# Attention and two MoE layers on one core: first loads in smaller pieces, the first GEMM by column halves, a new order table

## The chip, the core and the metric

The kernel runs on one core of a Trainium2 chip. The metric is the device time of one execution in microseconds: 537.37 us before the change, the median of 3 runs (537.26 to 537.60). In the text PE is the matmul engine, DVE the vector engine, ACT the scalar engine, POOL GpSimd, and SP the engine that issues the DMAs.

## The reference

Three layers follow each other on 1152 tokens (2 batches of 576) of width 512.

```python
# attention: 8 heads of 64; heads 0-3 see 32 keys back, heads 4-7 every 4th of 128 keys back
attn = softmax(where(mask, q @ k.T / 8, -1e9)) @ v
# layer 1: w_in 512x1024 and w_out 1024x512, both float64
h = x @ w_in
solu = h * softmax(h)
x = (solu - mean) / sqrt(var + 1e-6) * g_ln @ w_out
# layer 2: 4 experts, w1 512x1024 and w2 1024x512, float32
out = sum_e p[:, e] * (relu(x @ w1[e]) @ w2[e])
```

## The kernel before

**Attention.** A unit is one batch and one third of the positions of 4 heads: P units for the plain mask, D units for the dilated one, 12 units in all. `att_U` (L238) works a unit in 12 steps. PE puts the mask and 24 small products into a PSUM tile `pa` (the scores, L245 and L254). DVE takes the maximum (L262) and subtracts it (L264), ACT takes the exponent (L267), DVE the sum (L269) and its reciprocal (L271), and POOL or DVE the product into `pd` (L273). PE transposes `pd` (L279), ACT or DVE copies it (`pt`), PE multiplies it with the values (AV, L292), and the result is split into a rounded part `xhi` and a rest `xlo` (L308, L311). A D unit needs a third of `qkD`, which one load of 1168 KB brings.

**Weights.** `load_in` brings float64 weights `w_in`; `conv_in` turns a piece into float32 and splits it into `wh` and `wl`: two ACT passes, three DVE or POOL passes (`convert`, L169), a cast (`copy`) and a subtraction (L206). `w_in` comes in 128-row pieces: `draw0` in two halves of 512 columns, the other three whole. `load_out` and `conv_out` do the same for `w_out`.

**The first GEMM.** `moe_H` (L315) multiplies 128 tokens with all 1024 columns: for each of 4 row pieces `kk` three products (hi*hi, hi*lo, lo*hi) on both column halves, 24 matmuls into one PSUM tile `pm`. DVE then takes the row maximum (`nmx`, L326), ACT the exponent, and so on; `moe_T` (L340) transposes, `moe_X` (L359) is the second GEMM. Two `pm` and two `pa` tiles exist. Layer 2 (`up`, `down`, from L486) is unrolled by loops at the end, whose order the change leaves alone.

**The order.** Every engine executes its instructions in the order of the code. Up to the first expert's half that order is written out in the table `ORDER`: each word takes one generator one step further (`UP.t.b` and `UD.t.b` units, `lP`, `lD`, `lvp`, `lvd` loads of q, k and v, `lI` and `VI` loads and conversions of `w_in`, `lO` and `VO` of `w_out`, `H`, `T`, `X` the GEMM steps). A `+` moves the step's free choices to other engines: in `copy` from ACT to DVE, in `pick` between DVE and POOL. All loads are issued by SP in that order; a load waits there when its buffer is in use or when one of 8 DMA queues still has the load of eight before.

**The end.** `down` (L539) computes 128 tokens of the result; the last tile is cut into two column pieces of 256, so that the first can be stored while the second is computed. Both pieces are halves of one PSUM tile `po`.

## Time and profile before

| | us |
|---|---|
| median of 3 runs | 537.37 |
| the profiled execution | 536.57 |
| its span, first to last instruction | 534.8 |
| around the span | 1.77 |
| PE busy | 520.2 |
| DVE busy | 349.6 |
| ACT busy | 198.9 |
| POOL busy | 166.8 |

The span is divided into 40 slices of 13.4 us on the page; PE is below nine tenths in the first one alone. The costs below come from the profiled execution, which is 0.80 us shorter than the median run. A timeline row gives start, duration, engine, line, the operation and what ended the idle time before it.

### The profile page before, as it was taken

The numbers are of one execution on the slowest core, as the hardware profiler recorded it, in microseconds if no ns is written. First come the engines' busy times: TensorE is split into PE (matmuls) and PEld (weight loads), VectorE is DVE, ScalarE is ACT, GpSimd is POOL, SyncE is SP. The second block draws the span as 40 slices with busy tenths as digits, with TensorE's granted clock in tenths as the row PEclk, the third lists the DMA queues.
The fourth block names the chain that finished last, engine by engine and source line by source line (L and its number), as shares of the span: only waits on it lengthen the run. The fifth ranks groups of instructions, "written<-read, shape, count | busy, mean of one in ns | idle before, by whom it ended". The sixth has DMA issues, their size and how long they took to land.

```text
span 534.8 us, 8713 instructions
## 1 busy us (share of the span) xinstructions
PE 520.2 (97%) x3660; PEld 465.8 (87%) x3660; DVE 349.6 (65%) x472; ACT 198.9 (37%) x302; POOL 166.8 (31%) x121
## 2 busy tenths in 40 slices
PE   4899999999999999999999999999999999999997
PEld 2668789889999898988989898898989889898986
DVE  6999995373889974865585386568538646853532
ACT  3877892445246231421332242133124213412200
POOL 3672320001002111731382173138217413820300
PEclk9999999999999999999999999999999999999999
DMA  8962140000132300500310040031005002000022
GB/s 326 406 214 101 64 135 1 0 1 20 60 132 65 119 2 0 159 1 0 98 60 1 1 157 1 0 102 58 1 1 158 0 1 79 1 1 0 2 80 97
DMA packets 16856, 36.21 MB, mean 68 GB/s; under 512 B 3376, under 2 KB 3632, under 8 KB 16176
## 3 DMA queue, kind: packets, MB, share of 16 engines
q1 hardware_dynamic: 16816, 35.65, 19.1%
q8 instruction: 29, 0.48, 0.4%
q14 instruction: 11, 0.09, 0.1%
HBM read 33.28 MB, written 2.36 MB: 67 GB/s over the span
## 4 chain that ended last, share of the span: by engine, by line
PE 94%; DMA 2%; DVE 2%; ACT 1%; issue 0%; SPq 0%; DVEq 0%; ACTq 0%
PE pm L553 18%; PE pa L553 18%; PE pm L483 17%; PE pa L483 17%; PE pm L321 10%; PE pm L370 8%; PE pa L292 2%; PE pa L349 2%; DMA draw<-in_moe_w_in_dram 2%; PE pa L279 1%; DMA rw<-in_moe_w_dram 1%; PE pa L254 1%; ACT pt L159 0%; DVE sm L264 0%; PE pa L245 0%
## 5 line engine op out<-in xcount | busy, mean ns | idle before, releaser
L496 DVE SCALAR_TENSOR_TENSOR hl<-ct,hh 128x512 fp32r<-128x512 f32 (+1 forms) x64 | 61.5, 980 | 32.4 <-ACT hh L494 32.4
L494 ACT ACTIVATE hh<-ct 128x512 fp32r<-128x512 f32 (+1 forms) x64 | 42.2, 682 | 51.9 <-DVE ct L526 22.9
L553 PE MATMUL pm<-wh,hh 128*128 128x512 f32 (+1 forms) x148 | 56.9, 384 | 0.6 <-DVE xf L558 0.6
L483 PE MATMUL pa<-xoh,hl 128*128 128x256 f32 (+1 forms) x192 | 56.9, 296 | 0.0
L483 PE MATMUL pm<-xoh,hl 128*128 128x256 f32 (+1 forms) x192 | 56.8, 296 | 0.0
L483 PE MATMUL pm<-xol,hh 128*128 128x256 f32 (+1 forms) x192 | 56.8, 296 | 0.0
L483 PE MATMUL pa<-xol,hh 128*128 128x256 f32 (+1 forms) x192 | 56.8, 296 | 0.0
L553 PE MATMUL pm<-wl,hh 128*128 128x512 f32 (+1 forms) x148 | 56.8, 384 | 0.0
L483 PE MATMUL pm<-xoh,hh 128*128 128x256 f32 (+1 forms) x192 | 56.8, 296 | 0.0
L483 PE MATMUL pa<-xoh,hh 128*128 128x256 f32 (+1 forms) x192 | 56.8, 296 | 0.0
L553 PE MATMUL pm<-wh,hl 128*128 128x512 f32 (+1 forms) x148 | 56.7, 383 | 0.0
L553 PE MATMUL pa<-wl,hh 128*128 128x512 f32 x144 | 56.1, 390 | 0.0
L553 PE MATMUL pa<-wh,hh 128*128 128x512 f32 x144 | 56.1, 390 | 0.0
L553 PE MATMUL pa<-wh,hl 128*128 128x512 f32 x144 | 56.0, 389 | 0.0
L510 POOL TENSOR_TENSOR ct<-ct,ct 128x512 f32<-128x512 f32 (+1 forms) x15 | 22.4, 1492 | 78.7 <-ACT ct L508 52.6
L402 POOL TENSOR_TENSOR wl<-wl,wh 128x1024 fp32r<-128x1024 f32 x7 | 16.9, 2413 | 95.7 <-ACT wh L159 95.7
L558 DVE SCALAR_TENSOR_TENSOR xf<-pm,pr,xf 128x512 f32<-128x512 f32 (+1 forms) x33 | 24.1, 730 | 32.9 <-PE pm L553 32.9
L159 ACT CAST wh<-wl 128x1024 fp32r<-128x1024 f32 x16 | 16.8, 1053 | 71.0 <-PE pa L553 40.6
L558 DVE SCALAR_TENSOR_TENSOR xf<-pa,pr,xf 128x512 f32<-128x512 f32 x31 | 23.1, 746 | 29.4 <-PE pa L553 29.4
L483 PEld LDWEIGHTS pm<-xoh,hh 128*128 128x128 f32 x192 | 36.4, 190 | 0.3
L483 PEld LDWEIGHTS pm<-xol,hh 128*128 128x128 f32 x192 | 36.4, 190 | 0.3
L483 PEld LDWEIGHTS pa<-xol,hh 128*128 128x128 f32 x192 | 36.4, 190 | 0.3
(180 smaller groups left out, 1252.6 us busy)
## 6 DMA issues: line engine op xcount, KB each, us to landing
wl<-in_moe_w_dram SPq DMA_DIRECT2D x16, 512.0 KB, 4.2
...
out_dram<-xf SPq DMA_DIRECT2D x8, 256.0 KB, 2.0
...
```

Source lines behind the costliest of these rows:

```text
L159: nc.scalar.copy(out, in_)
L292: nc.tensor.matmul(po[64 * row:64 * row + 64, 0, o:o + 96], lhsT=vv, rhs=pt[:, j, :, g, :], start=True, stop=True)
L321: nc.tensor.matmul(pm[:, n, :], lhsT=xx[:, kk, cols], rhs=ww["in", kk][:, 512 * n:512 * n + 512], start=(n_ == 0 and i < 2), stop=(n_ == K ...
L349: nc.tensor.transpose(pa[:, f // 4, (f % 4) * 128:(f % 4) * 128 + 128], e[:, f // 4, (f % 4) * 128:(f % 4) * 128 + 128], ident)
L370: nc.tensor.matmul(pm[:, dd, 0:CW], lhsT=w_, rhs=x_[:, f, :], start=(f == 0 and i == 0), stop=(f == KF - 1 and i == 2))
L402: pick().tensor_tensor(out=out, in0=a, in1=b, op=op)
L483: nc.tensor.matmul(ps[:, ff, 0:n], lhsT=a[:, kk, fc], rhs=b[:, kk, :], start=kk == 0 and m == 0, stop=kk == 1 and m == 2)
L494: nc.scalar.activation(out=hv, in_=src, func=AF.Relu)
L496: nc.vector.scalar_tensor_tensor(out=lv, in0=src, scalar=0.0, in1=hv.bitcast(F32), op0=ALU.max, op1=ALU.subtract)
L510: poolv().tensor_tensor(out=c12, in0=c21, in1=c22, op=ALU.add)
L553: nc.tensor.matmul(po[:, u, 0:dn], lhsT=h_[:, f, cols], rhs=w_, start=(f == 0 and i == 0), stop=(f == 3 and i == 2))
L558: nc.vector.scalar_tensor_tensor(out=acc[:, t, dc], in0=po[:, u, 0:dn], scalar=pr[:, t, e:e + 1], in1=acc[:, t, dc], op0=ALU.mult, op1=ALU ...
```

## The change

- Every load goes through `load`, which makes it wait until all but the last 2,000,000 bytes of the loads before it have landed.
- The q and k of D units come by thirds (459 KB each, overlap included), those of P units also by thirds; `w_in` comes in 8 pieces of 128x512 (524 KB each), each with buffers of its own; the converted pieces rotate through 4 buffers, the raw `w_out` pieces through 2.
- `moe_H` finishes columns 0 to 511 over all four `kk` before it begins columns 512 to 1023; a step is 3 matmuls instead of 6.
- `keep_busy` puts 4 bf16 matmuls of a zero tile, 512 columns each, behind the scores of the first P and the first D unit. The zero tile is set on DVE; the three `pd` tiles are set to zero on POOL instead of DVE.
- The last output tile is cut into 384 and 128 columns, in two PSUM tiles from different pools.
- `g_ln` and the expert weights `probs` are laid out by partition before the launch, so that their loads are no longer made of elements of 4 and 16 bytes.
- `ORDER` is another table.

```diff
-KORD = (0, 1, 2, 3)
-HCUT = (1, 1, 2, 2, 4, 2, 4, 4, 4)
-XCUT = (2, 2, 4)
+HCUT = (1, 1, 1, 1, 2, 2, 2, 4, 4)
+XCUT = (1, 1, 2)
 NEG = -8.0e9
+AHEAD = 2000000
...
-lI.0 lP.0.0 VI.0 lD.0 VI.0 UP.0.0 VI.0 UD.0.0 VI.0 UP.0.0 UP.0.0 UD.0.0 lI.4 lP.1.0 VI.4 UP.0.0 UD.0.0 UP.0.0 lI.1 UP.0.0 UD.1.0 UD.1.0 lI.2 VI.0+
...
+lP.0.0 UP.0.0 UP.0.0 UP.0.0 UP.0.0 UP.0.0 UP.0.0 lD.0.0 UD.0.0 wu.4 wu.4 wu.4 wu.4 UP.0.0 lI.3 VI.3 VI.3 UD.0.0 UD.0.0 UD.0.0 UP.0.0 UP.0.0
...
+    wz = const.tile([128, 512], BF16, name="wz")
+    nc.vector.memset(wz.bitcast(U32), 0)
+    wps = psm.tile([128, 2, 512], F32, name="pm", tag="pm")
...
-    cv = at.enter_context(tc.tile_pool(name="cv", bufs=1))
+    cvp = at.enter_context(tc.tile_pool(name="cvp", bufs=4))
+    crp = at.enter_context(tc.tile_pool(name="crp", bufs=2))
...
-    QP, QD = 2 * TH, 2 * S
+    QP, QD = 2 * TH, 4 * 96
...
-        qkD.append(p.tile([128, QD + 32 + 2 * S], F32, name=f"qkD{b}", tag=f"qkD{b}"))
+        qkD.append(p.tile([128, 3, QD + 4 * 128], F32, name=f"qkD{b}", tag=f"qkD{b}"))
...
-        nc.vector.memset(pd, 0.0)
+        nc.gpsimd.memset(pd, 0.0)
...
+    loads = []
+
+    def load(out, in_):
+        i = nc.sync.dma_start(out=out, in_=in_).ins
+        n = mybir.dt.size(out.dtype)
+        for d in out.shape:
+            n *= d
+        loads.append((i.name, n))
+        total = 0
+        for k in range(len(loads) - 1, -1, -1):
+            total += loads[k][1]
+            if total > AHEAD:
+                info = mybir.DependencyInfo(mybir.DependencyClass.Sync, mybir.DependencyReason.DATA)
+                tc.add_manual_dep(i, loads[k][0], info, reason="bytes on the way")
+                break
...
     def load_qk(quad, t, b):
         if quad == "D":
-            nc.sync.dma_start(out=qkD[b], in_=qkd[b])
+            load(out=qkD[b][:, t], in_=qkd[b, :, t])
         else:
-            ts = slice(0, 1) if t == 0 else slice(1, 3)
-            nc.sync.dma_start(out=qkP[b][:, ts], in_=qkp[b, :, ts])
+            load(out=qkP[b][:, t], in_=qkp[b, :, t])
...
+    def keep_busy(n):
+        for i in range(n):
+            nc.tensor.matmul(wps[:, i % 2, :], lhsT=wz[:, 0:128], rhs=wz, start=True, stop=True)
+            yield
...
     def load_in(j):
         j, half = j % 4, j // 4
-        if half:
-            nc.sync.dma_start(out=dins[j][:, 1024:2048].bitcast(I64), in_=w_in[128 * j:128 * j + 128, 512:1024])
-            return
-        r = dins[j] = erp.tile([128, 2048], I32, name=f"draw{j}", tag=f"draw{j}")
-        n = 512 if j == 0 else 1024
-        nc.sync.dma_start(out=r[:, 0:2 * n].bitcast(I64), in_=w_in[128 * j:128 * j + 128, 0:n])
+        r = dins[j, half] = erp.tile([128, 1024], I32, name=f"draw{j}{half}", tag=f"draw{j}{half}")
+        load(out=r.bitcast(I64), in_=w_in[128 * j:128 * j + 128, 512 * half:512 * half + 512])
 
     def conv_in(j):
         j, half = j % 4, j // 4
-        sl = slice(512 * half, 512 * half + (512 if j == 0 else 1024))
+        sl = slice(512 * half, 512 * half + 512)
         if ("in", j) not in whi:
             whi["in", j] = wp.tile([128, 1024], F32R, name=f"wh{j}", tag=f"wh{j}")
             wlo["in", j] = wp.tile([128, 1024], F32R, name=f"wl{j}", tag=f"wl{j}")
-        a = (erp.tile([128, 1024], F32, name="eva", tag="eva") if j % 2 else cva)[:, sl]
-        yield from convert(dins[j][:, 2 * sl.start:2 * sl.stop], a)
+        a = cvp.tile([128, 512], F32, name="cva", tag="cva")
+        yield from convert(dins[j, half], a)
...
     def load_out(j, t):
-        nc.sync.dma_start(out=cvr[:, 1024 * t:1024 * t + 1024].bitcast(I64), in_=w_out[256 * j + 128 * t:256 * j + 128 * t + 128, :])
+        r = douts[j, t] = crp.tile([128, 1024], I32, name="cvr", tag="cvr")
+        load(out=r.bitcast(I64), in_=w_out[256 * j + 128 * t:256 * j + 128 * t + 128, :])
...
-            qt, kt, hq, hk, mi = qkD[b][:, 0:QD], qkD[b][:, QD:], S // 2, S // 2, (1, 2, 0)[t]
+            qt, kt, hq, hk, mi = qkD[b][:, t, 0:QD], qkD[b][:, t, QD:], 96, 128, (1, 2, 0)[t]
...
-        for n_, kk in enumerate(KORD):
-            seq = [(xhi, whi, n) for n in range(2)] + [(xhi, wlo, n) for n in range(2)] + [(xlo, whi, n) for n in range(2)]
-            for i, (xx, ww, n) in enumerate(seq):
-                nc.tensor.matmul(pm[:, n, :], lhsT=xx[:, kk, cols], rhs=ww["in", kk][:, 512 * n:512 * n + 512],
-                                 start=(n_ == 0 and i < 2), stop=(n_ == KD - 1 and i >= 4))
-            if n_ % HCUT[t] == HCUT[t] - 1:
-                yield
+        for n in range(2):
+            for kk in range(KD):
+                for i, (xx, ww) in enumerate(((xhi, whi), (xhi, wlo), (xlo, whi))):
+                    nc.tensor.matmul(pm[:, n, :], lhsT=xx[:, kk, cols], rhs=ww["in", kk][:, 512 * n:512 * n + 512],
+                                     start=(kk == 0 and i == 0), stop=(kk == KD - 1 and i == 2))
+                if (n * KD + kk) % HCUT[t] == HCUT[t] - 1:
+                    yield
...
-        po = pair(g % 2 + t + (0 if t < 4 else 1))
-        cuts = ((0, 256), (256, 256)) if last and t == NTT - 1 else ((0, 512),)
+        k = g % 2 + t + (0 if t < 4 else 1)
+        cuts = ((0, 384), (384, 128)) if last and t == NTT - 1 else ((0, 512),)
...
+            po = pair(k + u)[:, 0, 0:dn]
...
-        nc.sync.dma_start(out=g_sb, in_=g_ln.rearrange("(f p) -> p f", p=128))
-        nc.sync.dma_start(out=pr_raw, in_=probs.rearrange("(t p) e -> p t e", p=128))
+        load(out=g_sb, in_=g_ln)
+        load(out=pr_raw, in_=probs.rearrange("p (t e) -> p t e", t=NTT))
```

The table's effect on the queues. PE at the very start; `pa` tiles hold scores, transposes and AV results, `wz` is the zero tile. Before:

```order
L254 MATMUL pa_163<-qkP0_103 32x64 x24
...
L254 MATMUL pa_191<-qkD0_104 32x64 x24
...
L254 MATMUL pa_233<-qkD0_104 32x64 x24
...
L254 MATMUL pa_272<-qkP0_103 32x64 x24
...
L254 MATMUL pa_309<-qkD0_104 32x64 x24
L279 MATMUL pa_339<-ident_69,pd0_109 128x128 x6
```

After:

```order
L282 MATMUL pa_160<-qkP0_109 32x64 x24
...
L282 MATMUL pa_194<-qkD0_110 32x64 x24
...
L172 MATMUL pm_71<-wz_69 128x512
L307 MATMUL pa_237<-ident_72,pd0_115 128x128 x6
...
L282 MATMUL pa_253<-qkP0_109 32x64 x24
L320 MATMUL pa_295<-pt_244,vp_291 64x96 x8
...
L282 MATMUL pa_313<-qkD0_110 32x64 x24
```

Before, five units' scores stand ahead of the first transposes; now two, with the zero matmuls between, and the first AV stands ahead of the fourth unit's scores.

DVE just ahead of the row maximum of token tile 0 (`nmx` from the tile's `pm`); `cva` and `eva` are converted pieces, `wl` their rests, `st` and `sm` belong to a unit's softmax. Before:

```order
L262 TENSOR_REDUCE st_664<-pa_594 128x6
L271 RECIPROCAL st_507<-st_507 128x6
L264 TENSOR_TENSOR sm2_114<-pa_594,st_664 128x6x64
L273 TENSOR_TENSOR pd0_109<-sm0_112,st_507 128x6x64
L231 TENSOR_TENSOR xlo_87<-pa_641,xhi_86 128x2x2x96
L271 RECIPROCAL st_621<-st_621 128x6
L326 TENSOR_REDUCE nmx_79<-pm_447 128x1
```

After:

```order
L290 TENSOR_REDUCE st_714<-pa_686 128x6
L292 TENSOR_TENSOR sm1_119<-pa_686,st_714 128x6x64
L231 TENSOR_TENSOR wl2_341<-cva_652,wh2_340 128x512
L188 CAST xhi_89<-pa_730 128x2x192
L259 TENSOR_TENSOR xlo_90<-pa_730,xhi_89 128x2x192
L297 TENSOR_REDUCE st_714<-sm1_119 128x6
L299 RECIPROCAL st_714<-st_714 128x6
L259 TENSOR_TENSOR xlo_90<-pa_748,xhi_89 128x2x192
L354 TENSOR_REDUCE nmx_82<-pm_460 128x1
```

Two more units' results stand ahead of that maximum now, and the last pieces of `w_in`. Counted over the whole queues up to that point:

| | before | after |
|---|---|---|
| PE up to tile 0's last matmul: units with scores / transposes / AV | 9 / 5 / 5 | 9 / 7 / 7 |
| PE: matmuls of tile 0, of tile 1, zero matmuls | 24, 12, 0 | 24, 18, 4 |
| DVE up to tile 0's maximum: first maximum, subtraction / sum, reciprocal | 9 / 8 | 9 / 8 |
| DVE: `xlo` subtractions (by units) / `xhi` casts / `pt` copies | 5 / 0 / 1 | 7 / 2 / 0 |
| DVE: half pieces of `w_in` through the first two passes | 8 | 8 |
| DVE: the third pass / `wh` cast / `wl` subtraction, in half pieces | 0 / 0 / 4 | 3 / 1 / 5 |
| DVE: zeroing of `pd` | 3 | 0 |

DVE at the handover from the first GEMM to layer 2; `hl` is the rest of a transposed tile that the last second-GEMM group needs, `ct` and `sw` are the first sums of layer 2. Before:

```order
L231 TENSOR_TENSOR hl_1419<-pa_1498,hh_1418 128x8x128
L402 TENSOR_TENSOR ct0_1581<-xf_1236 128x2x256
L402 TENSOR_TENSOR sw0_1590<-rw0_1543,rw1_1545 128x2x256
L231 TENSOR_TENSOR hl_1419<-pa_1489,hh_1418 128x8x128
L157 CAST hh_1586<-rw0_1543 128x512
```

After:

```order
L188 CAST hh_1443<-pa_1554 128x8x128
L259 TENSOR_TENSOR hl_1444<-pa_1554,hh_1443 128x8x128
L188 CAST hh_1443<-pa_1566 128x8x128
L259 TENSOR_TENSOR hl_1444<-pa_1566,hh_1443 128x8x128
L188 COPY xf_1313<-pm_1498 128x2x384
```

Before, a sum that reads a load of `w1` stands between the two `hl`; now each cast and its `hl` follow each other, and the loads' readers come later.

## Rows read from the trace of the kernel before

**Rows 1.** Windows: length, busy PE PEld DVE ACT POOL, PE clock, DMA share, GB/s.
```profile
6.47:40.56 34.09, 29.27 (x561) 20.92 (x549) 29.71 (x57) 23.82 (x36) 20.92 (x13) 1.00 0.87 327
40.56:94.70 54.14, 54.14 (x518) 46.67 (x517) 45.08 (x76) 37.54 (x60) 11.26 (x10) 1.00 0.22 74
135.00:140.00 5.00, 4.29 (x25) 3.97 (x24) 4.67 (x8) 1.75 (x2) 0.00 (x0) 1.00 0.18 67
...
0.00:30.00 30.00, 20.05 (x437) 14.28 (x438) 24.05 (x52) 18.90 (x27) 16.58 (x27) 1.00 0.95 371
30.00:130.00 100.00, 99.92 (x867) 85.59 (x866) 71.58 (x113) 61.00 (x94) 18.49 (x14) 1.00 0.18 56
```

**Rows 2.** Timeline of PE: scores, AV, transposes, scores, tile 0's last matmuls.
```profile
18.14 0.97 PE L254 MATMUL pa<-qkP 64*32 64x64 f32 x48
...
20.50 0.88 PE L292 MATMUL pa<-pt,vp 128*64 128x96 f32 x16
...
23.64 0.82 PE L279 MATMUL pa<-ident,pd 128*128 128x128 f32 x6
...
26.14 0.72 PE L254 MATMUL pa<-qkP 64*32 64x64 f32 x48
...
39.89 0.63 PE L321 MATMUL pm<-wh,xlo 128*128 128x512 f32 x2
```

**Rows 3.** Timeline of ACT and POOL: the first piece of w_in, first and last pass.
```profile
4.41 0.67 ACT L173 ACTIVATE draw<-draw 128x512 int32<-128x512 uint32 x1 [2.39 <-DMA draw<-in_moe_w_in_dram]
...
12.65 1.27 POOL L206 TENSOR_TENSOR wl<-cva,wh 128x512 fp32r<-128x512 f32 x1 [3.68 <-ACT wh L159]
```

**Rows 4.** DVE by line: count, ns minimum/median/maximum, first and last start; then its timeline.
```profile
L231 DVE TENSOR_TENSOR xlo<-pa,xhi x14: 497/546/887, 22.4 to 94.7; 128x384 fp32r<-128x384 f32 x10, 128x192 fp32r<-128x192 f32 x4
...
L157 DVE COPY pt<-pa x1: 957/957/957, 17.7 to 17.7; 128x768 f32<-128x768 f32 x1
...
L181 DVE CUSTOM_DVE_ANT_0 cva<-cvr,cva x3: 680/685/693, 74.7 to 82.9; 128x1024 uint16<-128x1024 uint16 x3
...
L206 DVE TENSOR_TENSOR wl<-eva,wh x1: 1210/1210/1210, 27.2 to 27.2; 128x1024 fp32r<-128x1024 f32 x1
...
6.47 0.36 DVE L177 TENSOR_SCALAR cva<-cva 128x512 uint32<-128x512 uint32 x1
...
10.17 0.56 DVE L262 TENSOR_REDUCE st<-pa 128x6 f32<-128x384 f32 x1 [1.56 <-PE pa L254]
...
14.31 0.68 DVE L177 TENSOR_SCALAR cva<-cva 128x512 uint32<-128x512 uint32 x1
...
40.56 1.22 DVE L326 TENSOR_REDUCE nmx<-pm 128x1 f32<-128x1024 f32 x1
```

**Rows 5.** The chain that ended last, two pieces; then PE's one wait there.
```profile
65.55 5.47 PE pm L321 x24
...
138.40 16.74 PE pm L370 x95
...
PE pm L370 <- DVE hl L231: 0.7, 1, 0.7
```

**Rows 6.** The end: transposes (chain), PE and DVE timeline, stores with us to landing.
```profile
127.44 1.76 PE pa L349 x16
...
527.69 0.28 PE L553 MATMUL pm<-wh,hh 128*128 128x256 f32 x1
527.89 0.75 DVE L558 SCALAR_TENSOR_TENSOR xf<-pa,pr,xf 128x512 f32<-128x512 f32 x1 [1.97 <-PE pa L553]
529.86 0.39 PE L553 MATMUL pm<-wh,hh 128*128 128x256 f32 x1 [0.58 <-DVE xf L558]
531.59 0.48 DVE L558 SCALAR_TENSOR_TENSOR xf<-pm,pr,xf 128x256 f32<-128x256 f32 x1 [1.78 <-PE pm L553]
...
out_dram<-xf SPq DMA_DIRECT2D x8, 256.0 KB, 2.0
out_dram<-xf SPq DMA_DIRECT2D x2, 128.0 KB, 1.7
```

More of the change, by code (lines that the diff above doesn't have):

```diff
@@ L141, in load_vp @@
         vps[u, b] = t
-        nc.sync.dma_start(out=t.rearrange("p c h d -> p (c h d)"), in_=vpw[b, :, u])
+        load(out=t.rearrange("p c h d -> p (c h d)"), in_=vpw[b, :, u])
+    def keep_busy(n):
+        for i in range(n):
+            nc.tensor.matmul(wps[:, i % 2, :], lhsT=wz[:, 0:128], rhs=wz, start=True, stop=True)
+            yield
     whi, wlo = {}, {}
@@ L165, in fused_kernel @@
     wpo = [None]
-    cvr = cv.tile([128, 2048], I32, name="cvr", tag="cvr")
-    cva = cv.tile([128, 1024], F32, name="cva", tag="cva")
     def convert(raw, a):
@@ L206, in conv_in @@
         pick().tensor_tensor(out=lo, in0=a, in1=hi.bitcast(F32), op=ALU.subtract)
+    douts = {}
     def load_out(j, t):
-        nc.sync.dma_start(out=cvr[:, 1024 * t:1024 * t + 1024].bitcast(I64), in_=w_out[256 * j + 128 * t:256 * j + 128 * t + 128, :])
+        r = douts[j, t] = crp.tile([128, 1024], I32, name="cvr", tag="cvr")
+        load(out=r.bitcast(I64), in_=w_out[256 * j + 128 * t:256 * j + 128 * t + 128, :])
     def conv_out(j, t):
         sl = slice(512 * t, 512 * t + 512)
-        a = cva[:, sl]
-        yield from convert(cvr[:, 1024 * t:1024 * t + 1024], a)
+        a = cvp.tile([128, 512], F32, name="cva", tag="cva")
+        yield from convert(douts[j, t], a)
         if ("out", j) not in whi:
@@ L388, in load_w1 @@
             r = r.rearrange("p (t f) -> p t f", t=2)
-            nc.sync.dma_start(out=r, in_=w1[e, 256 * kh:256 * kh + 256, 512 * fh:512 * fh + 512].rearrange("(t p) f -> p t f", p=128))
+            load(out=r, in_=w1[e, 256 * kh:256 * kh + 256, 512 * fh:512 * fh + 512].rearrange("(t p) f -> p t f", p=128))
             w1raw[g].append(r)
@@ L397, in load_w2 @@
             f0 = 512 * fh + 256 * j
-            nc.sync.dma_start(out=r, in_=w2[e, f0:f0 + 256, :].rearrange("(t p) f -> p t f", p=128))
+            load(out=r, in_=w2[e, f0:f0 + 256, :].rearrange("(t p) f -> p t f", p=128))
             w2raw[g].append(r)
@@ L487, in up @@
         _, n, _ = SCH[s]
-        hh, hl = hb[s]
         k = g % 2 + (s if g else 1 - s)
@@ L552, in down @@
                 for i, (h_, w_) in enumerate(((hh, wh), (hh, wl), (hl, wh))):
-                    nc.tensor.matmul(po[:, u, 0:dn], lhsT=h_[:, f, cols], rhs=w_, start=(f == 0 and i == 0), stop=(f == 3 and i == 2))
+                    nc.tensor.matmul(po, lhsT=h_[:, f, cols], rhs=w_, start=(f == 0 and i == 0), stop=(f == 3 and i == 2))
             yield
             if g == 0:
-                nc.vector.tensor_scalar(out=acc[:, t, dc], in0=po[:, u, 0:dn], scalar1=pr[:, t, e:e + 1], scalar2=None, op0=ALU.mult)
+                nc.vector.tensor_scalar(out=acc[:, t, dc], in0=po, scalar1=pr[:, t, e:e + 1], scalar2=None, op0=ALU.mult)
             else:
-                nc.vector.scalar_tensor_tensor(out=acc[:, t, dc], in0=po[:, u, 0:dn], scalar=pr[:, t, e:e + 1], in1=acc[:, t, dc],
+                nc.vector.scalar_tensor_tensor(out=acc[:, t, dc], in0=po, scalar=pr[:, t, e:e + 1], in1=acc[:, t, dc],
                                                op0=ALU.mult, op1=ALU.add)
@@ L689, in _lay_out @@
         d[name] = a[:, at].reshape(b, 128, 3, 8 * n)
+    d["moe_g_ln"] = d["moe_g_ln"].reshape(-1, 128).T
+    p = d["moe2_domain_probs"]
+    d["moe2_domain_probs"] = p.reshape(-1, 128, p.shape[1]).transpose(1, 0, 2).reshape(128, -1)
     return d
```

59 lines of the change are left out of this document (35 added, 24 removed).

## The prediction

> **What bounds the kernel now.** I read the windows first. Between 30 and 130 us PE is busy for 99.92 of 100 us, and the page's slices are full from there to the end; in the first 30 us it is busy for 20.05 [rows 1]. So the kernel is bound by PE, and a change that leaves PE's matmuls alone can win three things: the PE time lost at the start, a hole between 135 and 140 us (4.29 busy of 5.00) [rows 1], and what the last tile costs. The hole ends with PE waiting 0.7 us for a DVE subtraction that makes `hl` [rows 5]. At the end PE stands still for 0.58 us until DVE has read the first half of a PSUM tile whose other half it wants to write [rows 6].
>
> At the start PE waits for work that other engines make. Between 6.47 us, when DVE's first pass over a weight begins, and 40.56 us, when it takes tile 0's row maximum, DVE is busy for 29.71 of 34.09 us, more than PE (29.27), ACT (23.82) or POOL (20.92) [rows 1]. The DMA moved 371 GB/s over the first 30 us with a share of 0.95 [rows 1]: loads are nearly at their limit too. Afterwards, from 40.56 to 94.70, PE is never idle while DVE has 9.06 us left [rows 1]. So the size of the loss at the start is fixed by one question: how much has PE done when tile 0's GEMM ends, and when is that.
>
> **The start, step by step.** Before, tile 0's last matmul ends at 40.52 [rows 2] and its maximum starts at 40.56 [rows 4]. By then PE has behind it what the table of counts in the section on the change lists. After, up to the same matmul, PE's queue holds two transposes of units, two AV groups and 6 matmuls of tile 1 more. At 0.82 and 0.88 us a group [rows 2] and 5.47 / 24 = 0.228 us a matmul [rows 5] this is 1.64 + 1.76 + 1.37 = 4.8 us of PE work that is done earlier. If tile 0 ended at the same time, 4.8 us would be won; every us that it ends later takes one back.
>
> When does it end? DVE's queue tells. Up to the maximum it has the same 9 and 8 softmax steps and the same 8 half pieces in the first two passes, and against that: one `pt` copy less (-0.96), two `xlo` more (2 x 0.55), two `xhi` casts of the same shape (taken alike, 2 x 0.55), three third passes (3 x 0.69), a `wl` half piece more (half of 1.21, 0.61) and a `wh` cast of the same size (taken alike) [rows 4]. Together +4.5, so 29.71 + 4.5 = 34.2 us. It can start when the first scores are there. The first load before, 512 KB, was used at 4.41 [rows 3]; the first one now is 416 KB of q and k, so at the latest then, plus 0.97 for cold scores [rows 2]: 5.4. DVE's idle time in that stretch was 34.09 - 29.71 = 4.4; 1.56 of it was the wait for a D unit's scores [rows 4], whose 1168 KB now come by thirds, so I take 2.8. 5.4 + 34.2 + 2.8 = 42.4: tile 0 ends 1.85 later than before, and 4.8 - 1.85 = **2.9 us** are won. Ends: with 1 us of idle time 40.6 and 4.7 won, with the old 4.4 us 44.0 and 1.3 won.
>
> The loads allow this. The last half piece that tile 0 needs is the 25th load; by their sizes the 25 are 11.0 MB, and at 371 GB/s they are in at 30 us [rows 1]. From landing to the end of the last pass the first piece took 4.41 to 13.92, 9.5 us with its queues [rows 3]; 39.5 and a last step of 3 x 0.228 makes 40.2, before the 42.4. The 2,000,000 bytes are 5.4 us of that rate, more than the 4.41 us within which the first load was there [rows 3], so SP's new waits should not open holes; behind a waiting load stand only other loads.
>
> What I cost at nothing: the zero matmuls (4 x 512 columns, at most twice 0.228 each, 1.8 us) stand where PE waits for the first `pd`, which is five DVE and ACT steps behind the first scores; if that cover were gone they would cost up to 1.8 once. The three zeroings on POOL: POOL's first passes of before ended with waits such as 3.68 us [rows 3], and the first `pd` of a unit comes later than them. The granted clock is 1.00 (2.4 GHz) in every window, yet scores took 0.97 at 18.14 and 0.72 at 26.14 [rows 1, 2]. Keeping PE at work early may bring the short form sooner, but this shortens groups that wait for DVE anyway: nothing, and at most 0.25 us a scores group on the first units' own chains. The column halves themselves keep the number and size of the matmuls. The 4 and 16 byte loads vanish from SP's queue, where no early load stood behind them.
>
> **Later waits.** After tile 0, DVE's list up to the last `xlo` is almost of the same length as before, but it stands 1.85 us later while PE stands 2.9 us ahead. Before, DVE had 9.06 us to spare there [rows 1], most of it at the end. Where a `pm` or `pa` tile must be read by DVE before PE writes it again, PE will now wait. I take **-1.2 us**, between 0 (PE did not wait once before) and -2.9 (the lead is eaten).
>
> **The handover.** Now cast and `hl` of the last two tiles follow each other on DVE, four passes over 1024 columns, at the 1.22 of the row maximum [rows 4] 4.9 us, under 48 matmuls of 16.74 / 95 = 0.176 us, 8.5 us [rows 5]. The 0.7 us wait goes: **+0.7**. Next late would be layer 2's first operands; DVE is busy for 4.67 of 5 us there [rows 1], but by the order six of its passes go to POOL. End: 0.
>
> **The end.** Before, 3.90 us lie between the last tile's first matmul (527.69) and its last DVE step (531.59) [rows 6]. Now 12 x 0.176 = 2.11 for 384 columns, then 12 matmuls of 128 columns. No product here has 128; transposes of 128 columns take 1.76 / 16 = 0.110 [rows 6], so 11 x 0.110 and about 0.27 to the result: 3.60, 0.30 won. The DVE step shrinks from 0.48 by half of 0.75 - 0.48, 0.13; the store, from 2.0 at 256 KB and 1.7 at 128, by 0.15 [rows 6]. **+0.6**; bounds: a matmul in proportion to its columns, 0.067, gives 1.1; one as long as a 512-column one, 0.228, gives -0.7.
> The Trainium skill (TensorE: Matmul & The Clock Gate, "Back-to-back issue gap") gives about 81 ns for such a matmul in a stream; by that the end wins 0.9 instead of 0.6. But it also gives 131 ns for 512 columns where this trace shows 228, so I keep the row's value.
>
> **Sum.** 2.9 - 1.2 + 0.7 + 0.6 = 3.0 us: the profiled execution would go from 536.57 to 533.6, the median from 537.37 to **534.4 us**.
>
> **Rivals.** *POOL slows DVE.* The same half-piece pass on DVE took 0.36 us at 6.47 with POOL idle and 0.68 at 14.31 beside POOL [rows 4]. Eight of them at 0.68 are 2.6 us more: tile 0 ends at 45.0, 0.35 won at the start, nothing left to lose later: with 1.3 from the other terms 535.7. The same time results, 535.9, if the later waits eat the lead.
> The Trainium skill (SBUF — State Buffer, the rule on the shared port pair) says DVE and POOL lock a common port pair for a whole instruction, which agrees with the two rows and would make this rival the rule.
> *The last weights come late* (slower). Tiles 0 and 1 now both hold a `pm` tile until the second column halves of all pieces are there, so PE stands still when the 25th load is late, 1 us for 1 us. It decides from tile 0 ending at 42.4 + 2.9 + 1.3 = 46.6, that is from a landing at 36.4, an average of 0.30 MB/us. Against it: 371 GB/s and the slack of 2.2 us. For it: SP waits before every load now. A landing at 39 would give 540.0.
> *The narrow cut is dear.* 0.228 a matmul at the end: 535.7.
> *The start closes further.* DVE almost without gaps and no later waits: 4.7 + 0.7 + 0.6 = 6.0, 531.4.
>
> **How the numbers follow.** Forecast 0.50 (alone 532.5 to 536.0), POOL or later waits 0.18, late weights 0.12, narrow cut 0.08, closing further 0.12. 0.2% is 1.1 us, about what this kernel's measurement can tell from no change: the border is 536.3. Faster: 0.49 + 0.09 + 0.06 + 0.12 = 0.76; within: 0.01 + 0.09 + 0.02 = 0.12; slower 0.12. The range from 531.0 to 537.5 leaves out the late weights and the far end of the last rival.
>
> **What the new profile shows.** Right: tile 0's maximum between 40.6 and 44.0 with DVE busy from 5.4 on; PE without the wait for `hl` after the last transposes; no PE idle time inside the last tile, 3.6 us from its first matmul to its last DVE step. The later waits would show as PE waiting for DVE between 45 and 95 us. Wrong would be: ACT waiting for a `draw` load with tile 0 open, passes on DVE near 0.7 us throughout, or tile 0 ending later than 46.6.

## The result: 0.7% slower

The changed kernel takes 541.06 us (median of 4 runs, 539.92 to 542.12) where the kernel before took 537.32 beside it: a ratio of 1.0070, 95% interval 1.0048 to 1.0093. Forecast were 534.4 us and a range of 531.0 to 537.5: wrong sign and outside the range. The profiled execution took 541.2 us with a span of 539.4, against 536.57 and 534.8: 4.6 us more.

PE's busy time is what it was (520.5 us, before 520.2); what grew is the time in which it stands still. The windows of the changed kernel, cut at the row maximum of token tile 0 and at that of tile 8 (columns as in [rows 1]):

```profile
0.00:45.60 45.60, 34.32 (x651) 24.92 (x652) 37.44 (x82) 27.78 (x48) 20.37 (x34) 0.96 0.85 288
45.60:124.00 78.40, 76.45 (x601) 65.93 (x599) 61.55 (x93) 46.90 (x74) 9.00 (x9) 1.00 0.15 50
124.00:539.40 415.40, 409.72 (x2416) 375.15 (x2414) 259.44 (x310) 115.71 (x177) 150.10 (x93) 1.00 0.14 47
```

The same cut at the maxima of before:

```profile
0.00:40.56 40.56, 30.54 (x598) 21.86 (x599) 33.55 (x69) 26.32 (x39) 23.81 (x30) 1.00 0.84 312
40.56:120.33 79.77, 79.77 (x644) 68.37 (x643) 58.22 (x92) 49.47 (x77) 11.26 (x10) 1.00 0.15 51
120.33:534.80 414.47, 409.93 (x2422) 375.55 (x2420) 257.82 (x315) 123.12 (x186) 131.75 (x81) 1.00 0.14 47
```

Tile 0's maximum comes at 45.60 instead of 40.56, 5.04 us later. PE's work left from there is 76.45 + 409.72 = 486.2 us instead of 79.77 + 409.93 = 489.7, 3.5 less. PE's idle time from there is 1.95 + 5.68 = 7.6 us instead of 0 + 4.54, 3.1 more. 5.0 - 3.5 + 3.1 = 4.6.

Where PE waits, from the waits of the changed kernel (total, times, longest):

```profile
PE pa L273 <- ACT pt L190: 2.9, 1, 2.9
PE pa L282 <- DMA qkD<-in_qkd_dram: 2.1, 2, 1.1
PE pm L582 <- ACT ct L528: 1.3, 1, 1.3
PE pm L511 <- DVE ct L532: 1.0, 1, 1.0
PE pa L320 <- DVE pt L188: 0.6, 1, 0.6
PE pa L320 <- DVE xlo L259: 0.4, 1, 0.4
PE pa L377 <- DVE hl L259: 0.3, 1, 0.3
PE pm L582 <- DVE wl L430: 0.3, 1, 0.3
```

The first two lie ahead of tile 0's maximum. The waits for `pt`, `xlo` and the first GEMM's `hl` lie between 48 and 88 us, where before did not wait once. L511 and L582 are layer 2: PE stands still 1.04 us before 165.11 and 1.25 us before 176.54, places where before ran through. The wait for `hl` at the handover [rows 5] is gone.

**The start.** In ACT's timeline two weight passes wait for their load while tile 0 is open:

```profile
15.81 0.66 ACT L202 ACTIVATE draw<-draw 128x512 int32<-128x512 uint32 x1 [2.23 <-DMA draw<-in_moe_w_in_dram]
17.95 0.79 ACT L190 COPY pt<-pa 128x768 f32<-128x768 f32 x1
38.96 0.67 ACT L202 ACTIVATE draw<-draw 128x512 int32<-128x512 uint32 x1 [2.55 <-DMA draw<-in_moe_w_in_dram]
```

The copy of `pt` at 17.95, for which PE waits 2.9 us, stands in ACT's queue behind the pass that waited for the load. The DMA moved 295 GB/s between 10 and 30 us where it had moved 411.

**The end** did what was forecast. PE's and DVE's timelines at the last tile:

```profile
532.77 0.33 PE L582 MATMUL pm<-wh,hh 128*128 128x384 f32 x1
534.88 0.22 PE L582 MATMUL pa<-wh,hh 128*128 128x128 f32 x1
536.06 0.28 PE L582 MATMUL pa<-wh,hl 128*128 128x128 f32 x1
536.37 0.35 DVE L587 SCALAR_TENSOR_TENSOR xf<-pa,pr,xf 128x128 f32<-128x128 f32 x1 [0.67 <-PE pa L582]
```

From the first matmul to the last DVE step it is 536.37 - 532.77 = 3.60 us; before it was 3.90 [rows 6].

### The profile page after: what moved, and what is told of

Same layout as the page of the kernel before. It is cut to its first block, busy times and chain, and to the rows that moved or that the text cites. A ratio compares the mean times of both kernels' runs of the same rounds, so it can differ in the third digit from the quotient of the medians.

```text
span 539.4 us, 8761 instructions
## 1 busy us (share of the span) xinstructions
PE 520.5 (96%) x3663; PEld 466.0 (86%) x3664; DVE 358.4 (66%) x483; ACT 190.4 (35%) x299; POOL 179.5 (33%) x135
## 3 DMA queue, kind: packets, MB, share of 16 engines
HBM read 33.64 MB, written 2.36 MB: 67 GB/s over the span
## 4 chain that ended last, share of the span: by engine, by line
PE 75%; DVE 14%; DMA 7%; issue 2%; ACT 1%; POOL 0%; DVEq 0%; POOLq 0%; ACTq 0%
PE pa L582 18%; PE pm L582 18%; PE pm L511 15%; PE pa L511 15%; PE pm L349 5%; DMA qkD<-in_qkd_dram 4%; PE pm L398 3%; DMA qkP<-in_qkp_dram 2%; DMA draw<-in_moe_w_in_dram 1%; DVE e L358 1%; DVE hl L259 1%; DVE nmx L354 1%; DMA vd<-in_vdw_dram 1%; PE pa L377 1%; DVE hl L430 1%
## 5 line engine op out<-in xcount | busy, mean ns | idle before, releaser
L524 DVE SCALAR_TENSOR_TENSOR hl<-ct,hh 128x512 fp32r<-128x512 f32 (+1 forms) x64 | 63.8, 1017 | 36.2 <-ACT hh L522 36.1
L511 PE MATMUL pm<-xoh,hh 128*128 128x256 f32 (+1 forms) x192 | 56.9, 297 | 1.0 <-DVE ct L532 1.0
L582 PE MATMUL pa<-wl,hh 128*128 128x512 f32 (+1 forms) x148 | 57.2, 387 | 0.0
L582 PE MATMUL pm<-wh,hh 128*128 128x512 f32 (+1 forms) x144 | 56.0, 389 | 1.3 <-ACT ct L528 1.3
L582 PE MATMUL pa<-wh,hh 128*128 128x512 f32 (+1 forms) x148 | 57.2, 386 | 0.0
L582 PE MATMUL pa<-wh,hl 128*128 128x512 f32 (+1 forms) x148 | 57.1, 386 | 0.0
L511 PE MATMUL pa<-xoh,hl 128*128 128x256 f32 (+1 forms) x192 | 56.9, 296 | 0.0
L511 PE MATMUL pm<-xoh,hl 128*128 128x256 f32 (+1 forms) x192 | 56.9, 296 | 0.0
L511 PE MATMUL pa<-xol,hh 128*128 128x256 f32 (+1 forms) x192 | 56.9, 296 | 0.0
L511 PE MATMUL pm<-xol,hh 128*128 128x256 f32 (+1 forms) x192 | 56.8, 296 | 0.0
L511 PE MATMUL pa<-xoh,hh 128*128 128x256 f32 (+1 forms) x192 | 56.8, 296 | 0.0
L582 PE MATMUL pm<-wl,hh 128*128 128x512 f32 (+1 forms) x144 | 56.0, 389 | 0.3 <-DVE wl L430 0.3
L582 PE MATMUL pm<-wh,hl 128*128 128x512 f32 (+1 forms) x144 | 55.8, 388 | 0.0
L587 DVE SCALAR_TENSOR_TENSOR xf<-pa,pr,xf 128x512 f32<-128x512 f32 (+1 forms) x32 | 23.5, 733 | 30.1 <-PE pa L582 30.1
L190 ACT CAST wh<-wl 128x1024 fp32r<-128x1024 f32 x16 | 16.8, 1052 | 71.0 <-PE pa L582 40.6
L430 POOL TENSOR_TENSOR hl<-sw,hh 128x512 fp32r<-128x512 f32 x20 | 30.0, 1501 | 24.7 <-ACT hh L190 24.7
L511 PEld LDWEIGHTS pm<-xoh,hh 128*128 128x128 f32 x192 | 36.4, 190 | 1.5 <-DVE ct L532 1.2
L511 PEld LDWEIGHTS pm<-xol,hh 128*128 128x128 f32 x192 | 36.4, 190 | 0.3
```

The costliest lines, as they stand in the source:

```text
L190: nc.scalar.copy(out, in_)
L430: pick().tensor_tensor(out=out, in0=a, in1=b, op=op)
L511: nc.tensor.matmul(ps[:, ff, 0:n], lhsT=a[:, kk, fc], rhs=b[:, kk, :], start=kk == 0 and m == 0, stop=kk == 1 and m == 2)
L524: nc.vector.scalar_tensor_tensor(out=lv, in0=src, scalar=0.0, in1=hv.bitcast(F32), op0=ALU.max, op1=ALU.subtract)
L582: nc.tensor.matmul(po, lhsT=h_[:, f, cols], rhs=w_, start=(f == 0 and i == 0), stop=(f == 3 and i == 2))
L587: nc.vector.scalar_tensor_tensor(out=acc[:, t, dc], in0=po, scalar=pr[:, t, e:e + 1], in1=acc[:, t, dc], op0=ALU.mult, op1=ALU.add)
```

## The experiments

Two theories were first to be told apart. L: the 2 MB limit starves the start. T: the new order of layer 2's first operands costs the time. The profile of each run has the same three pieces: when tile 0's maximum starts (A), from there to tile 8's maximum (B), and from there to the end of the span (C). Since each piece belongs to one part of the program, they tell apart what an edit does:

| run | A | B | C | median us | ratio to before, 95% |
|---|---|---|---|---|---|
| before | 40.6 | 79.8 | 414.5 | 537.32 | |
| the change | 45.6 | 78.4 | 415.4 | 541.06 | 1.0048 to 1.0093 |
| c1_after | 46.4 | 78.3 | 415.5 | 540.35 | 1.0049 to 1.0077 |
| c2_after | 44.1 | 78.3 | 415.5 | 539.71 | 1.0035 to 1.0062 |
| e1_no_limit | 43.4 | 78.3 | 415.5 | 539.44 | 1.0025 to 1.0055 |
| e2_limit_4mb | 43.8 | 78.3 | 415.5 | 539.08 | 1.0025 to 1.0052 |
| e3_no_zero | 43.8 | 78.3 | 415.5 | 539.65 | 1.0028 to 1.0061 |
| e4_old_layer2 | 44.0 | 78.3 | 412.2 | 536.38 | 0.9978 to 0.9997 |
| e5_before_tail | 41.1 | 79.8 | 414.0 | 536.68 | 0.9979 to 0.9997 |
| e6_open_old2 | 43.6 | 78.3 | 412.1 | 535.94 | 0.9974 to 0.9992 |
| e7_open_nozero_old2 | 43.7 | 78.3 | 412.1 | 536.09 | 0.9972 to 0.9989 |
| e8_products_first | 44.1 | 78.3 | 415.3 | 539.21 | 1.0026 to 1.0052 |
| e9_late_relief | 43.8 | 84.0 | 412.2 | 540.85 | 1.0054 to 1.0087 |
| e10_limit_1mb | 63.3 | 78.2 | 412.2 | 555.20 | 1.0320 to 1.0364 |
| e11_both_relief | 49.8 | 83.0 | 412.1 | 546.51 | 1.0159 to 1.0189 |
| e12_no_pool_layer2 | 44.0 | 78.3 | 419.0 | 542.45 | 1.0091 to 1.0121 |
| e13_one_pass_dve | 44.2 | 78.3 | 414.3 | 538.08 | 1.0014 to 1.0036 |
| e14_pt_on_act | 43.4 | 79.3 | 412.1 | 538.13 | 1.0009 to 1.0043 |
| e15_open_one_pass | 43.6 | 78.3 | 414.3 | 538.37 | 1.0013 to 1.0031 |
| e16_copy_first | 43.8 | 78.3 | 414.3 | 538.13 | 1.0014 to 1.0032 |

B and C hardly move unless an edit is made in them. (They are to be compared among the kernels with the new table, and before with e5: in the two tables tile 8's maximum stands at different places of PE's list.) A does: with the limit at 2 MB it lay between 43.8 and 46.4 in eight profiles, without it between 43.4 and 43.8 in seven (e11 aside, which has an edit of its own there).

**The limit.** One number changes: `AHEAD = 2000000` becomes 1000000000 (e1), 4000000 (e2), or 1000000 (e10, in the kernel of e4). The controls c1 and c2 are the changed kernel itself.

> The changed kernel with the limit on bytes on the way lifted (1 GB instead of 2 MB), everything else the same. Theory L (the limit starves the start): between 10 and 30 us the DMA moves 400 GB/s again as before the change, instead of 228 to 363; tile 0's row maximum starts at 42 to 43.5 us instead of 45.6, PE's idle time up to 45 us falls from 11.3 us to 8 or 9, and the time falls by 2 to 3 us to 538 to 539. Theory O (the new order itself stalls: ACT stands in front of a weight piece while a pt copy that PE wants is queued behind it): the rate comes back, but PE still waits about 3 us for ACT's pt copy near 18 us, the maximum stays later than 44.5 and the time stays at 540.5 to 541.5. A third outcome: with everything on the way at once the first loads share the engines and land later; then the first scores come later than 4.1 us and the time rises above 541.5.

> The changed kernel with the limit at 4 MB instead of 2 MB. Theory L: the limit binds less, the rate between 10 and 30 us is 350 to 400 GB/s and most of what the lifted limit gives is there: 538.5 to 539.5. Theory O: 540.5 to 541.5, as with the limit lifted. If late first loads are the cost of an open queue, 4 MB is better than no limit.

> The changed kernel with the old order of layer 2 and the limit at 1 MB instead of 2 MB. With 2 MB on the way the DMA moved 268 to 384 GB/s between 10 and 30 us, with no limit 400. If the rate follows the bytes on the way, 1 MB gives 150 to 220 GB/s; the 11 MB that tile 0 needs are then in at 50 to 65 us, tile 0's maximum starts at 55 us or later, and the time is 545 to 560. If a load's time from issue to landing shrinks with fewer on the way (6 us now), the rate stays above 250 GB/s and the time is 537 to 541.

> The changed kernel once more, unchanged, as a control beside the next three: its first profile had tile 0's maximum at 45.6 us and a granted clock of 0.74 and 0.92 between 15 and 25 us, while the run with the old order of layer 2, whose start is the same code, had 44.0 us and a clock of 1.00. If the start differs from one execution to the next, the time here spreads over 1 us or more and its median lies between 539 and 541; if the limit costs the same in each, the maximum is again at 45 to 46 us and the time at 541.

> The changed kernel once more as a control beside the next two. Its two profiles had tile 0's maximum at 45.6 and 46.4 us, five kernels with the same limit and the same or nearly the same start had 43.8 to 44.2, six without the limit or with 4 MB 43.4 to 43.8. If the limit makes the start differ from execution to execution, this profile can lie anywhere from 43.8 to 46.5 and the times spread over 2 us, median 540 to 541. If it lies at 45.5 or later again, something else than chance holds up the unchanged program's start.

Windows of the DMA, first with no limit, then of the change, then with 1 MB:

```profile
10.00:30.00 20.00, 15.21 (x355) 11.59 (x333) 18.67 (x40) 15.72 (x29) 8.81 (x9) 1.00 1.03 403
```
```profile
10.00:30.00 20.00, 14.00 (x327) 10.52 (x308) 16.88 (x36) 13.99 (x25) 8.70 (x8) 0.91 0.89 295
```
```profile
10.00:30.00 20.00, 13.15 (x257) 9.85 (x258) 13.81 (x28) 10.18 (x18) 6.62 (x6) 0.58 0.73 224
```

The rate follows the bytes on the way: 224, 295 and 403 GB/s; 4 MB give 403 too. With 1 MB tile 0 ends 19 us later than in e4 (63.3 and 44.0), as theory L had it. From 2 MB up the price is small and changeable: the limit's removal brought 539.44, the three runs of the unchanged program gave 541.06, 540.35 and 539.71. That is 0.3 to 1.6 us, less than L's 2 to 3; it shows where a load happens to be late. In c1 one D unit's scores waited 2.8 us for their load and A was 46.4, in c2 no wait for a load was over 0.2 us and A was 44.1. So L holds for the rate, and gives less than half of the loss (1.6 of 3.7 us at most, 0.3 of 2.5 for c2). Of theory O little is left: PE's wait for that copy of `pt` is 1.7 us in e1 and 1.0 to 1.2 in e2, c1 and c2, and the maximum came before 44.5 in all of them but c1.

**The zero matmuls** (the four `wu.4` out of the table: e3 in the changed kernel, e7 in that of e6).

> The changed kernel without the four zero matmuls. By the prediction they are hidden behind the first units' way through DVE and ACT: the time stays within 0.5 us of 541.1. A theory Z, that they hold up the first transposes (which came 0.2 us after pd was ready): 0.2 to 1 us less. A theory C, that they keep the granted clock up: the share at 1.2 GHz, now seen between 15 and 25 us, moves earlier and the first 25 us take 0.5 to 1.5 us longer.

> The same without the zero matmuls. By itself their removal won about 1 us, which the prediction did not have. If they hold up the first units, 0.5 to 1 us less than the run with them (534.5 to 535.5); if that gain was only another execution's start, the same within 0.4 us; if they keep the granted clock up, 0.3 to 1 us more, with a clock below 1.00 between 10 and 20 us.

536.09 in e7 beside 535.94 in e6: nothing, as predicted. e3's 539.65 lies just below the 539.71 to 541.06 of the unchanged program.

**Layer 2's first operands** (e4). From the word `endH` on, the table of before takes the place of the new one; its remaining steps of `T` are left out, since they are done by then, and the last entry of `XCUT` is the old 4.

> The changed kernel up to the point after the last tile's transposes; from there on the old kernel's order of steps (preparation of layer 2's first operands, first products). Theory T (the new order of layer 2's first operands makes PE wait 0.9 us near 164 us and 1.7 us near 177 us, where the kernel before did not wait): these waits vanish and 2 to 2.6 us are won, 538.5 to 539. Rival: DVE is the limit there (9 of 10 us between 150 and 180), the waits move to another place, and less than 1 us is won, 540 to 541.

Windows of e4; the idle time in layer 2 is gone:

```profile
95.00:165.00 70.00, 70.00 (x417) 66.06 (x416) 49.84 (x69) 27.98 (x42) 4.12 (x2) 1.00 0.16 53
165.00:200.00 35.00, 35.00 (x227) 32.83 (x226) 31.72 (x46) 13.65 (x22) 6.26 (x4) 1.00 0.14 46
```

536.38 us: 3.3 to 4.7 less than the three runs of the unchanged program, and C is 3.2 us shorter. That is as much as the whole loss, and it lies after the places where the prediction had looked for one. POOL is busy for 6.26 us between 165 and 200; in the change it was 21.46. With the limit lifted as well (e6):

> The changed kernel with the limit lifted and with the old order of layer 2's first operands: both of the edits that won by themselves. Theory: the gains add (1 to 2 us for the limit, 2.6 us for the order): 535 to 536. Rival: DVE, later in the list, eats the earlier start, and the time stays at that of the old order alone, 536.4.

535.94 us, 0.9983 of before: the smallest median of all runs and faster than both kernels. The second edit's 0.4 us lies within the two intervals.

**Which mechanism in layer 2?** First a repair by hand (e8): the first two products' steps ahead of DVE's passes for the second token group.

```diff
-XQ.1 XQ.1 XQ.1 XQ.1 XQ.1+ XQ.1 u.0 XQ.1+ u.0 u.0 u.0 u.0
+XQ.1 XQ.1 u.0 u.0 u.0 u.0 u.0 XQ.1 XQ.1 XQ.1+ XQ.1 XQ.1+
```

> The changed kernel, its own order, with one local repair: the first five steps of the first layer-2 product chain (its first two products, the copy and the addition that read them) stand ahead of five of the seven DVE passes of the second token group's operands, and no longer behind them. Theory Q (PE waits near 164 us because DVE runs six of those passes, 4.9 us, ahead of the addition that frees PE's PSUM tile, and near 177 us because the delayed chain holds up ACT's copy of the next one): the 1.0 us wait near 164 goes and the 1.2 us wait near 177 shrinks; 1 to 2.2 us less than the control's 540.4, so 538.2 to 539.4. Rival: the passes are only later, the second group's products wait for them, and less than 0.5 us is won.

The wait near 164 us went, and C stayed at 415.3: three of the next group's products (12 matmuls each) took 1.96 to 2.20 us instead of 1.76. The weight loads ahead of the matmuls now waited for DVE's additions, which read the PSUM tile that the next product wants:

```profile
167.51 0.19 PEld L511 LDWEIGHTS pa<-xoh,hh 128*128 128x128 f32 x1 [0.43 <-DVE ct L548]
169.47 0.19 PEld L511 LDWEIGHTS pm<-xoh,hh 128*128 128x128 f32 x1 [0.21 <-DVE ct L554]
171.46 0.19 PEld L511 LDWEIGHTS pa<-xoh,hh 128*128 128x128 f32 x1 [0.23 <-DVE ct L560]
```

So less than 0.5 us was won, as the rival had it, though by another wait. What lengthens DVE's list, its and POOL's timelines of the change show in part:

```profile
139.83 2.36 DVE L617 SCALAR_TENSOR_TENSOR nmx<-nmx,esq 128x9 f32<-128x9 f32 x1 [2.00 <-POOL esq L616]
166.55 2.02 DVE L524 SCALAR_TENSOR_TENSOR hl<-ct,hh 128x512 fp32r<-128x512 f32 x1 [0.70 <-ACT hh L522]
168.49 0.68 DVE L548 TENSOR_TENSOR ct<-pa,ct 128x512 f32<-128x512 f32 x1
169.20 1.35 DVE L550 TENSOR_TENSOR ct<-ct,ct 128x512 f32<-128x512 f32 x1
170.48 0.68 DVE L554 TENSOR_TENSOR ct<-pm,ct 128x512 f32<-128x512 f32 x1
171.85 0.69 DVE L524 SCALAR_TENSOR_TENSOR hl<-ct,hh 128x512 fp32r<-128x512 f32 x1 [0.70 <-ACT hh L522]
```
```profile
139.76 2.41 POOL L430 TENSOR_TENSOR xol<-xf,xoh 128x1024 fp32r<-128x1024 f32 x1
166.45 1.57 POOL L430 TENSOR_TENSOR xol<-sw,xoh 128x640 fp32r<-128x640 f32 x1
167.98 2.03 POOL L430 TENSOR_TENSOR sw<-xf 128x640 f32<-128x640 f32 x1
169.97 2.02 POOL L430 TENSOR_TENSOR sw<-xf,sw 128x640 f32<-128x640 f32 x1
```

A DVE pass over 9 columns takes 2.36 us, as long as the POOL pass beside it. e13 puts that one POOL pass back on DVE (the fourth step of `XQ.0` loses its `+`), e12 all 13 POOL passes from `endH` to the loops:

```diff
 def pick():
-    return nc.gpsimd if alt[0] != late[0] else nc.vector
+    return nc.gpsimd if alt[0] != late[0] and not nop[0] else nc.vector
```

> The changed kernel with one single pass back from POOL to DVE: the 1024-column subtraction for the first token group that ran on POOL from 139.8 to 142.2 us. Theory P: the 9-column pass beside it takes 0.2 us instead of 2.36, DVE's list gains 2.2 and pays 1.1 for the pass, and PE's wait near 164 us falls by about 1 us: time 0.5 to 1 us less than the control, 539.5 to 540.2. Rival: the 9-column pass is long for another reason (it waits for POOL's power function before it), stays at 2.4 us, and the time rises by up to 1 us.

> The changed kernel, its own order and limit, but from the end of the first layer to the start of the steady loop every pass that went to POOL (13 of them, 1.3 to 2.4 us each) stays on DVE. Theory P (a POOL pass holds up the DVE pass beside it: a DVE pass over 9 columns took 2.36 us beside a 2.41 us POOL pass and 0.17 without, others 2.02 and 1.78 instead of 0.69): DVE takes the six passes up to 177 us itself for some 5 us and gets back the 4.6 us or so of stretched passes, and POOL's longer chains go; PE's waits at 164 and 177 us shrink by 1 to 2.6 us, so 538 to 539.5 beside the control's 540.4 to 541.1. Rival (DVE's list is too long by itself there): the waits stay or grow, 540.5 to 543.

DVE's timeline of e13:

```profile
138.40 0.17 DVE L617 SCALAR_TENSOR_TENSOR nmx<-nmx,esq 128x9 f32<-128x9 f32 x1 [2.00 <-POOL esq L616]
141.51 1.22 DVE L430 TENSOR_TENSOR xol<-xf,xoh 128x1024 fp32r<-128x1024 f32 x1
```

PE's waits in layer 2 of e13:

```profile
PE pm L582 <- ACT ct L528: 1.3, 1, 1.3
PE pm L582 <- DVE wl L430: 0.3, 1, 0.3
```

0.17 instead of 2.36, at the price of 1.22: the wait near 164 us is gone and C is 1.1 us shorter; the median is 538.08. One pass that POOL "took over" had cost DVE more than it would have needed for it. But POOL is not just harm: with all 13 on DVE, C is 419.0, and PE waits for DVE's list:

```profile
PE pm L513 <- DVE xol L432: 2.9, 1, 2.9
PE pm L513 <- DVE xf L587: 2.0, 1, 2.0
```

Theory P holds for this one pass; for all 13 the rival does: taken together, POOL's passes save DVE more than they cost it. The two small edits together, and then one more move, the copy L528 ahead of two weight casts on ACT:

```diff
-u.0 WV.0 WV.0 XQ.1+ lW.2 XQ.1+ XQ.1+ XQ.1 WV.0 XQ.1 u.1 u.1 XQ.1 XQ.1+
+u.0 u.1 u.1 WV.0 WV.0 XQ.1+ lW.2 XQ.1+ XQ.1+ XQ.1 WV.0 XQ.1 XQ.1 XQ.1+
```

> The changed kernel, its own order, with just two small edits: no limit on bytes on the way, and the one 1024-column pass back from POOL to DVE. If these two are what made the change slower (by themselves they gave 539.4 and 538.1): 536.5 to 537.7, the time of the kernel before within 0.2%. If they overlap, 538.

> The same with one more move: the copy on ACT that frees the PSUM tile of the second group's first product stands ahead of two weight casts on ACT instead of behind them. Theory: PE's wait of 1.25 us near 174 us for that copy goes, the 0.33 us for wl behind it may stay or grow: 0.5 to 1.3 us less than the run without it. Rival: the casts, now later, hold up the second product instead (wh is wanted by the same matmuls): within 0.4 us of it.

e15 gave 538.37, not 537: against e13 the lifted limit brought nothing that can be measured. In e16 the wait for the copy went and came back as one for DVE's `wl`, C unchanged:

```profile
PE pm L582 <- DVE wl L430: 1.5, 2, 0.8
```

What is left, 2.1 us of C between these and the old order, was not taken apart. Passes of 2.02 and 1.35 us beside POOL stand in DVE's list in e16 too. And the old order puts one of DVE's two `wl` passes far ahead, at 158.84 in e4, where e16 has both behind the second group's operands; first e4, then e16:

```profile
158.84 1.22 DVE L430 TENSOR_TENSOR wl<-wl,wh 128x1024 fp32r<-128x1024 f32 x1
```
```profile
172.03 1.22 DVE L430 TENSOR_TENSOR wl<-wl,wh 128x1024 fp32r<-128x1024 f32 x1
174.43 1.22 DVE L430 TENSOR_TENSOR wl<-wl,wh 128x1024 fp32r<-128x1024 f32 x1
```

Which of the two it is, or whether it is something else in the order, is not shown.

**The waits between 45 and 95 us.** Starting from e6, e9 moves four third passes of `w_out` from DVE to POOL (a `+` at the fifth step of `VO.2.1`, `VO.2.0`, `VO.1.0`, `VO.3.1`) and two copies of `pt` to ACT (no `+` at the ninth step of `UP.2.1`, `UP.1.1`). e11 does that and moves four passes over `w_in` to POOL (`+` at the fifth step of `VI.5`, `VI.6`, the seventh of `VI.0`, `VI.2`). e14 has the two copies alone.

> The run with the limit lifted and the old order of layer 2 (535.9), with some of DVE's work between 55 and 92 us given away: the third pass of four half pieces of w_out goes to POOL, which stands idle there, and two copies of pt go to ACT. Theory: DVE's list is what makes PE wait between 45 and 95 us (1.85 us in five waits), and the waits for pt (0.64), xlo (0.4) and hl (0.3) shrink: 0.6 to 1.2 us less, 534.7 to 535.3. Rival: POOL's longer pass (1.3 instead of 0.69 us) delays the conversions and the waits come back at the next tile: within 0.4 us of 535.9.

> As the run with DVE relieved between 55 and 92 us, and relieved at the start as well: the third pass of two half pieces of w_in and the last pass of two others go from DVE to POOL (four passes of 0.69 us). By the prediction's own reckoning DVE's list sets when tile 0 ends: its maximum comes 2 to 2.8 us earlier than 43.6 us, at 41 to 41.6, and the time falls by 1 to 2 us more (533.5 to 534.5). Rival (POOL slows DVE, and its passes take 1.3 us): the conversions end later, tile 0's maximum stays at 43 or later and nothing or less than 0.5 us is won.

> The run with the limit lifted and the old order of layer 2 (535.9), with only the two late copies of pt given from DVE to ACT and nothing to POOL. In the run that gave passes to POOL as well, PE waited 4.5 us for a pd on POOL, which stood in POOL's queue behind a pass whose input came late. Theory: without POOL in it the relief works, the waits for xlo and pt (1.05 us) shrink, 0.4 to 1 us less, 535.0 to 535.5. Rival: ACT's queue now holds them up the same way: 535.9 to 538.

All three made it worse. PE's, then POOL's timeline of e9:

```profile
82.53 1.54 PE L307 MATMUL pa<-ident,pd 128*128 128x128 f32 x6 [4.51 <-POOL pd L301]
```
```profile
79.96 1.28 POOL L210 TENSOR_TENSOR cva<-cva,cvr 128x512 uint32<-128x512 uint32 x1 [8.36 <-DVE cva L208]
81.20 1.27 POOL L301 TENSOR_TENSOR pd<-sm,st 128x384 f32<-128x384 f32 x1
```

The `pd` for which PE waits 4.51 us stands in POOL's queue behind a pass whose input DVE made only at 79.96. So it is in e11 at the start too (a wait of 2.8 us for `wl` on POOL, part of the 6.2 us by which A grew to 49.8). In e14 one copy of `pt` came late on ACT: PE waited 1.72 us for it, 0.65 in e6 for the same copy on DVE. That is e14's 1.0 us of B; its profiled execution, 536.61, is one of the shortest of ten (536.58 to 540.60, at mean granted clocks from 1.00 down to 0.987), so where the median's 2.2 us come from is not in the trace. DVE is not simply the engine with too much to do there (44 of 50 us): what counts is what stands ahead in the queue that the work is moved to.

**The end by itself** (e5): in `down` of the kernel before, the cuts become 384 and 128 columns and each piece gets a tile.

```diff
-        po = pair(g % 2 + t + (0 if t < 4 else 1))
-        cuts = ((0, 256), (256, 256)) if last and t == NTT - 1 else ((0, 512),)
+        k = g % 2 + t + (0 if t < 4 else 1)
+        cuts = ((0, 384), (384, 128)) if last and t == NTT - 1 else ((0, 512),)
...
+            po = pair(k + u)[:, 0, 0:dn]
```

> The kernel before with only the last tile's new cut (384 and 128 columns, each in a PSUM tile of its own). In the changed kernel the way from the last tile's first matmul to the end of the span took 6.63 us instead of 7.11. Theory: the same here, 0.5 us less than before (0.9991 of it); PE's wait for the DVE step inside the last tile (0.58 us) is gone. Rival: the narrow matmuls or the extra store take it back, 0 to +0.3 us.

536.68 beside 537.20, 0.9988 of it: 0.5 us won, as expected, and C is 414.0 instead of 414.5.

## Why the prediction was wrong, step by step

| term | predicted | profiled execution |
|---|---|---|
| start | +2.9 | -0.6 |
| later waits | -1.2 | -1.95 |
| handover: wait for `hl` | +0.7 | +0.7 |
| what is late next | 0 | -3.2 |
| end | +0.6 | +0.5 |
| sum | +3.0 | -4.6 |

**What is late next** is the step that failed. "DVE is busy for 4.67 of 5 us there, but by the order six of its passes go to POOL. End: 0" put the term at nothing. It was 3.2 us, by e4: 2.6 are PE's waits (1.04 near 164 us for DVE's `ct`, 1.25 and 0.31 near 177 for ACT's `ct` and DVE's `wl`), the rest is in PE's busy time, 409.72 in C and 409.07 in e4. Not all of POOL's passes were relief: one held up a pass on DVE and cost 1.1 us of the 3.2 (e13). As a whole they were (e12), and still DVE's list in the new order was late; what makes up the other 2.1 us stays open. The rival *POOL slows DVE* had the mechanism of the first part and two rows with it [rows 4], but was laid out for the start only.

**The start.** Right was the begin of DVE's list (5.4 expected, 5.10 measured), and DVE is busy for most of the stretch; that its list alone decides was not shown, since e11, which shortened it, lengthened POOL's. Between there and tile 0's maximum the list was 35.8 us long, not 34.2, since half pieces of `wl` took 0.75 instead of 0.61 and the other passes were a little longer. DVE's idle time was 4.7 us, not 2.8; with the limit lifted it is 2.7, so that step failed by "SP's new waits should not open holes": 2 MB are 5.4 us of the full rate, but a 512 KB load took 6.4 us from issue to landing. The lead of 4.8 us was nearly right. PE's work left from tile 0's maximum is 76.47 + 409.07 = 485.5 us in e4, where layer 2 has no waits, 4.2 less than before, and the last tile's new cut adds 0.3 to PE's time: 4.5. So the start lost 5.04 - 4.46 = 0.6 us. With the limit lifted tile 0 comes at 43.4, and 4.5 - 2.8 = 1.7 us would be won instead of 2.9. The section on the profile before has PE below nine tenths in the first slice alone; on the page it is so in the first two and the last.

**Later waits**: the mechanism and its place were right; the 1.95 us of idle time lie within the bounds given, above the value taken. **The handover** and **the end** came out as worked out, the end to the hundredth (3.60 us; 0.111 us for a 128-column matmul, taken at 0.110). The bound of 0.067 us for such a matmul is not in proportion to its columns (0.176 / 3 is 0.059), but the bound's 1.1 us come out with either.

The rival *the last weights come late* showed its sign, ACT waiting for a `draw` load, but tile 0 ended before its border of 46.6, and lifting the limit won 0.3 to 1.6 us. The zero matmuls cost nothing, as assumed; the zeroing on POOL and the column halves were not tried by themselves. The granted clock was not 1.00 throughout, which is told below.

Chances of 0.76 for faster rested on terms that were each reasoned forward from DVE's rows. None asked for the whole of layer 2's new order what had been asked for the start: how long is DVE's list up to the point where PE wants it.
